# Second attention layer: QKV groups of the first chunk by half-step 5, transpositions of the second chunk in even half-steps

## The chip, the cores and the metric

The kernel runs on one core of a Trainium2 chip. The metric is device microseconds of one execution; "before" and "after" are medians of several runs on one chip. All times in this text are microseconds (us) unless another unit stands beside them.

Engine names are those of the profile: PE (matrix multiplication), DVE (vector), ACT (scalar), POOL (GpSimd), SP (the queue that issues most DMAs).

## The reference

Four layers in a row, each with a residual, on x of 2048 positions by 640 features:

```python
x = x + A(layernorm(x), wqkv, wo)      # attention
x = x + B(layernorm(x), dft matrices)  # Fourier mixing
x = x + A(layernorm(x), wqkv, wo)
x = x + B(layernorm(x), dft matrices)

def A(x, wqkv, wo):                    # 32 heads of 20 features
    q, k, v = split(x @ wqkv)
    # position s sees s, s-2, ..., s-14 (8 positions, dilation 2)
    logits = einsum("bhsd,bhswd->bhsw", q, k[idx]) * scale   # masked where idx < 0
    o = einsum("bhsw,bhswd->bhsd", softmax(logits), v[idx])
    return o @ wo

def B(x, ...):                         # real part of a DFT over features and positions
    a = x @ hid_re.T;  b = x @ hid_im.T
    return seq_re @ a - seq_im @ b
```

The weights are the same in both attention layers.

## The kernel before

Positions are split into four chunks `c` of four tiles `j` of 128 rows. The two attention layers are made by one function, `layer_a`; `first` is true in the first of them. Matrix products are made in three passes of split operands (a high part and a remainder), so each normalized tile has a high and a low half.

An attention layer is a plan of **half-steps**, from -7 to 66. One half-step computes one half (two position tiles, `jp`) of one attention unit `u`. A unit is one chunk and four heads (in the last chunk the two halves of a unit are two such sets of heads for the same two tiles): 32 units, 64 half-steps, half-step s = 2u + jp. For each, DVE multiplies Q by the eight shifted K rows (`qk_mul`, L431), POOL adds halves (L433), DVE reduces (L439) and makes the softmax with ACT's exponential (L447); three half-steps later DVE multiplies by V (`av_mul`, L469) and POOL adds the products up (L484 to L486).

PE meanwhile makes Q, K and V for later units. The work is cut in 64 **QKV groups** `g`, each of them 15 matmuls for one chunk, one quarter `q` of the heads and one tile `j` (`qkv_mm`, L362). ACT evacuates each (`qkv_evac`, L369) from one of two PSUM banks into a staging tile, of which there are two for pairs of groups; SP stores pairs to DRAM (`qkv_store`, L378 and L379), from where `w_load` (L417) and `q_load` (L401) fetch K and V windows and Q for the attention units. ACT copies Q to PSUM in each odd half-step (`q_copy`, L404).

Before a chunk's groups can run, its tiles of x are loaded (`x_load`, L195), in the first layer also reduced to mean and variance on ACT (`x_stats`, L151, L153, L170) with a power on POOL (`x_fin`, L174); then ACT normalizes (`x_norm`, L182 and L191) and PE transposes (`tp`: transposition L327, ACT's copy of the high half L331, PE's subtraction L335, ACT's copy of the low half L350). A tile of chunk c reuses the buffer of the same tile of chunk c-1, so it waits for the last group of that tile.

The order is written out by hand: `at(step, phase, fn, ...)` puts each operation into a half-step and one of some thirty phases, and the plan is issued half-step by half-step, phase by phase. Each engine, SP's queue too, works through its instructions in that order. Of the phases these matter here, in order: `peT0` (transpositions), `dma` (Q loads, x loads), `evac`, `hi`, `pe` (a group), `peL` (subtractions), `pe2` (a second group), `fin`, `red0`, `qk`, softmax phases, `exp`, `evacA`, `actL` (low halves), `evacO`, `actl` (normalizations), `av1`, `qc` (the Q copy), `actz`, `dmaw` (window loads), `dmas`, `misc`.

The half-steps of groups and transpositions come from a planner: the first 16 groups (chunk 0) from a list by hand, `LEAD0` for the first layer and `LEAD2` for the second; the others, and the half-steps `tx` of the transpositions, by a loop over half-steps with a cap on groups in each.

Between the attention layers lie the two Fourier layers, and the second attention layer begins while the first Fourier layer ends: that layer's last products (`ymm`, L1028) stand in half-steps -3 and -2.

Of the kernel before, what the change touches and what calls it, by code (L numbers as in the profile page):

```python
# [27 lines left out]
NC = 4  # L28
NJ = 4
# [13 lines left out]
LNS = ((40, 52), (40, 52))  # L43


LEAD2 = (-7, -6, -5, -4, -2, -1, 0, 0, 1, 2, 3, 4, 4, 5, 6, 7)
ZTHIRDS = (
    {49: 3, 50: 3, 51: 2, 53: 3, 54: 1, 56: 3, 57: 6, 58: 3, 59: 4, 60: 2, 61: 1, 62: 3, 63: 4, 64: 1, 55: 0, 52: 0},
    {49: 3, 50: 3, 51: 3, 52: 1, 53: 1, 54: 1, 55: 1, 56: 4, 57: 4, 58: 3, 59: 3, 60: 1, 61: 1, 62: 4, 63: 2, 64: 4},
# [25 lines left out]
def tile_layers(ctx: ExitStack, tc: tile.TileContext, x, wqkv, wo, cs, wre, wim, out):  # L75
# [166 lines left out]
    def layer_a(li, stats, handoff, prev):  # L242
        xin, xout = xs[li], xs[li + 1]
        first = li == 0
# [19 lines left out]
        def at(step, phase, fn, *args):  # L264
            plan.setdefault((step, phase), []).append((fn, args))
# [32 lines left out]
        def tp(step, kind, c, j, k0, k1, bank, col=0, tag=None):  # L298
            if step not in pieces:
                pieces[step] = []  # L300
                at(step, "peT0", pc_pe, step)
                at(step, "hi", pc_hi, step)
                at(step, "peL", pc_sub, step)
                at(step, "actL", pc_lo, step)
            pieces[step].append((kind, c, j, k0, k1, bank, col, tag))
# [387 lines left out]
        ]  # L693
        gs = list(LEAD0 if first else LEAD2)
        tx = {(0, j): -8 for j in range(NJ)}
        st = 4
        while len(gs) < NGRP:
            if (st % 2 == 0 if first or st > 10 else st > 4 and st != 6) and len(tx) < NC * NJ:
                c, j = divmod(len(tx), NJ)
                used = [i for i, x in enumerate(order) if x[0] == c - 1 and x[2] == j]  # L700
                if used[-1] < len(gs) and gs[used[-1]] < st:
                    tx[(c, j)] = st
            cap = 0 if st < 6 else 2 if st % 2 == 0 and st not in THIN[ly] else 1
            for _ in range(max(0, cap - gs[:16].count(st))):
                if len(gs) < NGRP and len(gs) <= 16 + st and tx.get(order[len(gs)][::2], st) < st:
                    gs.append(st)
            st += 1
        for g, cqj in enumerate(order):
            st = gs[g]
# [26 lines left out]
        for c in range(1, NC):  # L736
            for j in range(NJ):
                b = tx[(c, j)]
                if first or c > 1:
                    at(max(b - 4, tx.get((c, j - 2), 0)), "dma", x_load, c, j)  # L740
                else:
                    at((0, 1, 2, 3)[j], "dmas", x_load, c, j, ("xa", "xa", "xr", "ot")[j])
                if first:
                    at(b - 3, "actz", x_stats, c, j)
                    at(b - 2, "misc", x_fin, c, j)
                at(b - 1, "actl", x_norm, c, j)
                tp(b, "x", c, j, 0, 4, "xt", 0, f"s{j}")
                tp(b, "x", c, j, 4, 5, "t1", 256)
# [538 lines left out]
    st0 = [None] * NC  # L1287
    b1, b2 = LayerB(1), LayerB(3)
    layer_a(0, st0, b1, None)
    st2 = [None] * NC  # L1290
    b1.run(st2)
    layer_a(2, st2, b2, b1)
    b2.run(None)
    b2.ytile(NT - 1, 0, None)
# [56 lines left out]
```

## Time and profile before

| | |
|---|---|
| median of 3 runs | 1807.35 us (1806.6 to 1809.34) |
| the profiled execution | 1809.7 us, span of the trace 1807.9 us |
| busy: PE, DVE, ACT, POOL | 1750.4, 1387.8, 813.1, 633.4 us |
| share of the span | 97%, 77%, 45%, 35% |
| granted clock of TensorE, mean | 0.991 |
| QKV groups, both layers (L362) | 1920 matmuls, 441.3 us |
| Q copies of ACT (L404) | 64, median 431 ns |

The page's busy times are of one profiled execution. A group of instructions stands with its line, its engine, output and input tiles, and a count; in timelines the first number is the start in us from the start of the span, the second the duration, and a bracket at the end gives the idle time of the engine ahead of the instruction and what ended it. A wait for several things is put down to the last of them.

### The profile page before, as it was taken

What the parts mean: (1) busy time and instruction counts of PE and PEld (TensorE: products, weight loads), DVE (VectorE), ACT (ScalarE), POOL (GpSimd) and SP (SyncE); (2) the same over time, 40 slices, a digit from 0 to 9 for tenths busy, and PEclk for the clock granted to TensorE, in tenths of its full rate; (3) what the DMA queues carried; (4) which work ended last, traced back from release to release, by engine and by line L of the source; (5) the groups of instructions that cost most, each with busy time, mean ns of one, the idle gap of its engine ahead of it and who ended that gap; (6) DMA issues with size and microseconds to landing.
All of it is one profiled execution on the core that took longest, in us unless ns stands there. A gap on an engine that the chain in (4) does not pass through costs nothing.

```text
span 1807.9 us, 26461 instructions
## 1 busy us (share of the span) xinstructions
PE 1750.4 (97%) x8798; PEld 1508.4 (83%) x8798; DVE 1387.8 (77%) x2141; ACT 813.1 (45%) x1690; POOL 633.4 (35%) x591
## 2 busy tenths in 40 slices
PE   9999998989999999999998999999999999999999
PEld 7889887878888888888897888877787888888888
DVE  6999999787767767767736998999777676677673
ACT  4664544454445444445623334444534443443441
POOL 4889998940000000000016987999300000000000
PEclk9999998999999999999999999999999999999999
DMA  7996678758778788778645966697687776876761
GB/s 245 289 300 213 199 208 261 263 174 293 260 259 272 241 261 261 243 255 257 197 137 157 281 191 216 194 315 260 208 298 252 255 234 215 267 232 226 257 209 52
DMA packets 271849, 425.15 MB, mean 235 GB/s; under 512 B 22592, under 2 KB 150592, under 8 KB 271456
## 3 DMA queue, kind: packets, MB, share of 16 engines
q1 hardware_dynamic: 268512, 421.49, 71.8%
q10 hardware_dynamic: 3200, 1.97, 0.3%
q8 instruction: 70, 1.15, 0.3%
q14 instruction: 67, 0.55, 0.1%
HBM read 338.23 MB, written 85.14 MB: 234 GB/s over the span
## 4 chain that ended last, share of the span: by engine, by line
PE 42%; DVE 7%; DMA 5%; POOL 3%; ACT 1%; issue 1%; SPq 0%; DVEq 0%; ACTq 0%; POOLq 0%
PE aux L1028 10%; PE m L362 8%; PE t L1117 7%; PE m L1117 7%; PE pq L1117 4%; PE xt L1117 4%; DMA xc<-stg 2%; DVE pr L431 1%; DVE pr L469 1%; PE aux L509 1%; DMA win<-cs_in 1%; POOL pr L484 1%; POOL pr L433 1%; DVE lg L439 1%; POOL pr L485 0%
## 5 line engine op out<-in xcount | busy, mean ns | idle before, releaser
L362 PE MATMUL m<-r,s 128*128 128x480 f32 x1920 | 441.3, 385 | 6.9 <-ACT stg L369 4.0
L362 PEld LDWEIGHTS m<-r,s 128*128 128x128 f32 x1920 | 358.0, 190 | 63.3 <-ACT stg L369 6.0
L1110 ACT CAST r<-win 128x512 fp32r<-128x512 f32 x248 | 151.1, 619 | 172.9 <-DVE win L1146 83.6
L174 POOL TENSOR_TENSOR stats<-stats,mhalf 128x1 f32<-128x1 f32 (+1 forms) x40 | 29.8, 744 | 561.5 <-ACT stats L170 552.3
L1028 PE MATMUL aux<-r2a,zo 128*128 128x320 f32 x768 | 226.4, 310 | 0.0
L484 POOL TENSOR_TENSOR pr<-pr 128x640 f32<-128x640 f32 x126 | 204.5, 1623 | 34.9 <-DVE pr L469 34.1
L431 DVE TENSOR_TENSOR pr<-pq,win 128x1280 f32<-128x1280 f32 x128 | 189.7, 1483 | 26.6 <-ACT pq L404 26.0
L1028 PE MATMUL aux<-pr,zo 128*128 128x320 f32 x704 | 208.2, 308 | 0.0
L1111 DVE TENSOR_TENSOR r<-win,r 128x512 fp32r<-128x512 f32 x248 | 167.3, 687 | 45.6 <-ACT r L1110 44.4
L469 DVE TENSOR_TENSOR pr<-pq,win 128x1280 f32<-128x1280 f32 x128 | 190.9, 1491 | 4.3
L433 POOL TENSOR_TENSOR pr<-pr 128x640 f32<-128x640 f32 x128 | 183.2, 1431 | 29.6 <-DVE pr L431 29.3
L1117 PE MATMUL m<-r,r 128*128 128x512 f32 x606 | 157.2, 394 | 0.5 <-DVE r L1111 0.5
L1028 PEld LDWEIGHTS aux<-r2a,zo 128*128 128x128 f32 x768 | 144.2, 188 | 2.0
L1117 PEld LDWEIGHTS m<-r,r 128*128 128x128 f32 x606 | 114.0, 189 | 26.8 <-DVE r L1111 1.5
L1028 PEld LDWEIGHTS aux<-pr,zo 128*128 128x128 f32 x704 | 132.2, 188 | 2.1
L950 PE MATMUL m<-s,r 128*128 128x512 f32 x384 | 120.1, 400 | 14.1 <-DMA s<-c0b 5.5
L1117 PE MATMUL t<-r,r 128*128 128x512 f32 x483 | 131.0, 394 | 2.2 <-issue 2.2
L950 PE MATMUL t<-s,r 128*128 128x512 f32 x384 | 119.5, 399 | 2.3 <-DVE ot L1010 1.5
L485 POOL TENSOR_TENSOR pr<-pr 128x320 f32<-128x320 f32 x126 | 114.3, 907 | 9.9
L439 DVE TENSOR_REDUCE lg<-pr 128x64 f32<-128x640 f32 x128 | 103.9, 812 | 16.4 <-POOL pr L433 16.1
L1117 PEld LDWEIGHTS t<-r,r 128*128 128x128 f32 x483 | 90.6, 188 | 23.7 <-issue 3.0
L1146 DVE TENSOR_TENSOR win<-win,win 128x512 f32<-128x512 f32 x110 | 75.7, 690 | 43.9 <-DMA win<-cs_in 41.5
(284 smaller groups left out, 3228.6 us busy)
## 6 DMA issues: line engine op xcount, KB each, us to landing
win<-cs_in SPq DMA_DIRECT2D x354, 256.0 KB, 4.3
r<-xc SPq DMA_DIRECT2D x240, 256.0 KB, 4.4
win<-kvb SPq DMA_DIRECT2D x96, 440.0 KB, 4.3
xa<-cs_in SPq DMA_DIRECT2D x122, 256.0 KB, 4.1
win<-kvb SPq DMA_DIRECT2D x64, 360.0 KB, 5.3
xc<-stg SPq DMA_DIRECT2D x40, 512.0 KB, 3.6
kvb<-stg SPq DMA_DIRECT2D x60, 320.0 KB, 5.2
xr<-xs SPq DMA_DIRECT2D x41, 320.0 KB, 3.7
```

What stands on the lines that cost most here:

```text
L362: nc.tensor.matmul(mt[g][:, : 3 * F], st[:, a, k], wq[q][:, b, k], start=n == 0, stop=n == 14)
L431: nc.vector.tensor_tensor(pr, q, wview(u, jp, 0, [[1, FE]]), op=ALU.mult)
L433: nc.gpsimd.tensor_tensor(pv[:, :, 0:10], pv[:, :, 0:10], pv[:, :, 10:20], op=ALU.add)
L439: nc.vector.tensor_reduce(lgs[u][:, 2 * jp : 2 * jp + 2].rearrange("p j w h -> p (j w h)"), prq.pop((u, jp))[:, :, 0:10], axis=AX.X, op=AL ...
L469: nc.vector.tensor_tensor(pr.rearrange("p j w (h d) -> p j w h d", d=DH), lgs[u][:, 2 * jp : 2 * jp + 2].unsqueeze(4).to_broadcast([P, 2, ...
L484: g.tensor_tensor(pr[:, :, 0:4], pr[:, :, 0:4], pr[:, :, 4:8], op=ALU.add)
L485: g.tensor_tensor(pr[:, :, 0:2], pr[:, :, 0:2], pr[:, :, 2:4], op=ALU.add)
L950: self.last = nc.tensor.matmul(self.z[t][k], self.xn[c][:, a, j, k * P : (k + 1) * P], self.ct[s][:, b], start=s == 0 and i == 0, stop=s = ...
L1028: self.last = nc.tensor.matmul(self.ym[e][:, :320], zt[(k, a, ri)][:, j2 * P : (j2 + 1) * P], w[:, e * 320 : (e + 1) * 320], start=(k, a, ...
L1110: nc.scalar.copy(hi, raw)
L1111: nc.vector.tensor_tensor(lo, raw, hi.bitcast(F32), op=ALU.subtract)
L1117: nc.tensor.matmul(bank, w(a, kb), hl[b], start=start and (a, b) == (0, 0), stop=stop and (a, b) == (1, 0),)
```

## The change

```diff
-LEAD2 = (-7, -6, -5, -4, -2, -1, 0, 0, 1, 2, 3, 4, 4, 5, 6, 7)
+LEAD2 = (-7, -6, -5, -4, -2, -1, 0, 0, 1, 1, 2, 3, 3, 4, 5, 5)
...
         while len(gs) < NGRP:
-            if (st % 2 == 0 if first or st > 10 else st > 4 and st != 6) and len(tx) < NC * NJ:
+            if st % 2 == 0 and len(tx) < NC * NJ:
                 c, j = divmod(len(tx), NJ)
...
                 if first:
-                    at(b - 3, "actz", x_stats, c, j)
-                    at(b - 2, "misc", x_fin, c, j)
+                    at(b - 3, "actl", x_stats, c, j)
+                    at(b - 2, "fin", x_fin, c, j)
                 at(b - 1, "actl", x_norm, c, j)
```

In the second attention layer the planner's result becomes:

| | before | after |
|---|---|---|
| groups 8 to 15 in half-steps | 1, 2, 3, 4, 4, 5, 6, 7 | 1, 1, 2, 3, 3, 4, 5, 5 |
| transpositions of chunk 1 in | 5, 7, 8, 9 | 4, 6, 8, 10 |
| groups 16 to 25 in | 6, 8, 8, 9, 10, 10, 11, 12, 13, 14 | 6, 7, 8, 8, 9, 10, 10, 11, 12, 13 |
| groups 26 to 35 in | 14, 15, 16, 17, 18, 18, 19, 20, 21, 22 | 14, 14, 15, 16, 17, 18, 18, 19, 20, 21 |
| groups 36 to 63, other transpositions | | unchanged |

Normalizations lie one half-step ahead of a transposition and move with it; the x loads of chunk 1 stay in half-steps 0 to 3. The evacuation and the store of a group follow its half-step.

In the first attention layer groups and transpositions stay where they are. There the statistics of a tile (`x_stats`) move within their half-step from behind the Q copy to ahead of it, and the power on POOL (`x_fin`) from the end of its half-step, behind the additions, to ahead of them. This concerns the twelve tiles of chunks 1 to 3. No instruction is added or removed in either layer.

## The prediction

> **What bounds the kernel now.** I read the page first, then the chain of waits, then engine time by windows of 45 us, then the timelines of PE, DVE, ACT and the DMA queue around the edit. The edit lives in the two attention layers; the second runs from about 890 to 1290 us, and the window view shows what each engine does there against the first layer's 45 to 90 us.
>
> ```profile
> 45.00:90.00 45.00, 45.00 (x220) 38.75 (x219) 43.52 (x56) 27.86 (x67) 38.44 (x36) 1.00 0.91 288
> 950.00:995.00 45.00, 38.10 (x176) 31.76 (x176) 28.45 (x39) 15.90 (x36) 28.50 (x28) 0.96 0.51 156
> 995.00:1040.00 45.00, 44.78 (x217) 38.34 (x216) 43.64 (x58) 16.16 (x38) 42.09 (x39) 1.00 0.90 279
> 1085.00:1130.00 45.00, 45.00 (x244) 40.50 (x243) 38.14 (x58) 20.11 (x53) 35.27 (x33) 1.00 0.69 216
> ```
>
> The columns are busy us of PE, weight loads, DVE, ACT and POOL, then granted clock, DMA share and GB/s. The same work fills DVE with 43.52 of 45 us in the first layer's opening and only 28.45 of 45 in the second's (950 to 995); PE too drops there, to 38.10. After 995 DVE is full (43.64); by 1085 PE is full (45.00) and DVE sinks to 38.14. The chain of waits says who sets the end:
>
> ```profile
> 930.94 26.00 PE m L362 x120
> ...
> 1113.28 1.49 DVE pr L431
> ```
>
> From 931 on it runs over PE, mostly QKV groups (L362); at 1113 it changes to the DVE/POOL chain of the attention half-steps. So what counts for the edit is time in which PE stands still before 1113. PE's own timeline, with idle time and its releaser in brackets:
>
> ```profile
> 930.78 26.16 PE L362 MATMUL m<-r,s 128*128 128x480 f32 x120
> 957.24 3.50 PE L362 MATMUL m<-r,s 128*128 128x480 f32 x15
> 966.80 5.08 PE L362 MATMUL m<-r,s 128*128 128x480 f32 x15 [2.49 <-ACT stg L369]
> 973.40 0.66 PE L327 MATMUL xt<-ident,xa 128*128 128x128 f32 x4 [1.51 <-ACT xa L191]
> 979.34 0.66 PE L327 MATMUL xt<-ident,xr 128*128 128x128 f32 x4 [1.60 <-ACT xr L191]
> 992.62 7.64 PE L362 MATMUL m<-r,s 128*128 128x480 f32 x34 [1.25 <-ACT stg L369]
> 966.00:972.00 6.00, 5.08 (x15) 3.93 (x15) 5.15 (x7) 0.78 (x3) 5.49 (x5) 0.72 0.34 122
> ```
>
> Eight groups stream in 26.16 us (3.27 each), then PE waits 2.49, 1.51, 1.60 and 1.25 us, always for ACT (an evacuation L369, or a normalization L191 ahead of a transposition). Group 16 after the first wait takes 5.08 us, the one at 957.24 took 3.50, with the granted clock at 0.72. DVE has it worse; L431 is the QK product that opens each half-step:
>
> ```profile
> 949.46 1.49 DVE L431 TENSOR_TENSOR pr<-pq,win 128x1280 f32<-128x1280 f32 x1
> 962.13 1.49 DVE L431 TENSOR_TENSOR pr<-pq,win 128x1280 f32<-128x1280 f32 x1 [3.39 <-ACT pq L404]
> 979.64 1.49 DVE L431 TENSOR_TENSOR pr<-pq,win 128x1280 f32<-128x1280 f32 x1 [8.32 <-ACT pq L404]
> 992.94 1.49 DVE L431 TENSOR_TENSOR pr<-pq,win 128x1280 f32<-128x1280 f32 x1 [4.09 <-ACT pq L404]
> 1002.05 1.48 DVE L431 TENSOR_TENSOR pr<-pq,win 128x1280 f32<-128x1280 f32 x1
> ...
> 1077.09 0.49 DVE L159 SCALAR_TENSOR_TENSOR xr<-aux,xr 128x320 f32<-128x320 f32 x1 [1.98 <-PE aux L509]
> 1113.28 1.49 DVE L431 TENSOR_TENSOR pr<-pq,win 128x1280 f32<-128x1280 f32 x1 [1.50 <-ACT pq L404]
> ```
>
> These are half-steps 4, 6, 8, 10, 12, then two later rows. DVE stands 3.39 + 8.32 + 4.09 = 15.8 us, each time for L404, ACT's copy of Q. The reason stands on ACT, which works in order:
>
> ```profile
> 961.00 0.59 ACT L350 CAST s<-xt 128x512 fp32r<-128x512 f32 x1 [2.77 <-PE xt L335]
> 961.64 0.45 ACT L404 COPY pq<-qs 128x320 f32<-128x320 f32 x1
> ```
>
> L350 is the second evacuation of a transposition; it waits 2.77 us for PE's subtraction (L335), which stands behind a whole QKV group. The Q copy is issued in odd half-steps, and before the change the transpositions of chunk 1 sit in 5, 7, 9 (and 8): the copy queues behind L350, and DVE behind the copy.
>
> **The change, second layer.** I worked out the planner's list by hand from its code. After it, groups 9 to 15 lie one half-step earlier (15 two), transpositions of chunk 1 in 4, 6, 8, 10, and groups 17, 19, 20, 22 to 25 and most up to 35 one half-step earlier; from half-step 22 on the list is the old one. No instruction is added or removed; PE has the same work, in another order.
>
> What is removed: with the transpositions in even half-steps, L350's wait falls into a half-step without a Q copy, and group 15 no longer stands behind the transposition of (1,1). I walked PE and ACT through the new list with the durations above. PE enters at group 6 at 934.05 (930.78 + 3.27) and every bank it needs is evacuated, and every tile normalized, before PE arrives, with 0.5 us or more to spare, up to the transposition of half-step 20. So the four waits go: 2.49 + 1.51 + 1.60 + 1.25 = 6.85 us. The slow group goes too: 5.08 - 3.50 = 1.58. Together **8.4 us off PE's stretch**.
>
> The clock term is where a rule is weighed. The row: 2.49 us of waiting were followed by a group at granted clock 0.72. By the Trainium skill (TensorE: Matmul & The Clock Gate, "HAM oscillation") PE drops to the slow clock only after gaps above some 3.4 us, and by that rule the 1.58 us were not this gap's and would stay, the saving then being 6.85 us. The trace disagrees, so the sum keeps the term.
>
> What is late next. DVE's 15.8 us do not all come off: in my walk half-step 12 starts at 994.2 instead of 1002.05 (7.9 us earlier), since PE is the bound from half-step 1 on. From 1002 to 1060 DVE goes at its own pace and only then falls behind PE (waits such as 1.98 us for PE at 1077.09, 1.50 for ACT at 1113.28), so PE's 8.4 and DVE's 7.9 arrive at half-step 34 nearly together; I take 8.4, PE being what ended last there. Behind 1113 the list is unchanged and the shift passes to the end.
>
> What is added: in half-steps 1 and 3 two groups stand where one stood. Their evacuations come ahead of the exponential on ACT, and the store of group 9 comes ahead of the load of the next K window on the DMA queue, which is in order as well:
>
> ```profile
> 944.88 0.43 SPq L417 DMA_DIRECT2D win<-kvb  x1
> 947.78 0.37 SPq L378 DMA_DIRECT2D kvb<-stg  x1
> 46.23 0.64 SPq L417 DMA_DIRECT2D win<-kvb  x1
> 52.11 1.49 DVE L431 TENSOR_TENSOR pr<-pq,win 128x1280 f32<-128x1280 f32 x1 [0.21 <-DMA win<-kvb]
> ```
>
> The second-layer window load issued at 944.88, ahead of group 9's store at 947.78; with the new list it comes behind it, as in the first layer, where the load issued at 46.23 and the product waited for it until 52.11. I expect half-step 4 at about 954 instead of 949.46, 4.5 us late. I cost this at nothing, because in that stretch PE has queued groups to work on (it does not wait for half-step 4 before group 13's bank, evacuated by then) and DVE regains it in half-steps 6 to 10 where 15.8 us of waits lay. If that cover is gone, it costs up to 4.5. Store and evacuation of the staged pairs keep their two buffers: each is reused two pairs later, 6.5 us (2 x 3.27) on at the least.
>
> **The change, first layer.** The planner gives the same list there. What moves are the statistics of x: two ACT passes from behind the Q copy to ahead of it, and the POOL power (L174) from the end of the half-step to its start. Twelve tiles each.
>
> ```profile
> 51.21 0.43 ACT L404 COPY pq<-qs 128x320 f32<-128x320 f32 x1 [1.09 <-DVE pr L469]
> 51.57 0.73 ACT L151 ACTIVATE junk<-xa 128x640 bf16<-128x640 f32 x1
> 53.39 0.20 ACT L170 ACTIVATE stats<-stats 128x1 f32<-128x1 f32 x1
> 71.23 0.30 ACT L182 ACTIVATE stats<-stats 128x1 f32<-128x1 f32 x1 [0.39 <-POOL stats L174]
> 72.39 0.42 ACT L404 COPY pq<-qs 128x320 f32<-128x320 f32 x1
> 73.80 1.47 DVE L431 TENSOR_TENSOR pr<-pq,win 128x1280 f32<-128x1280 f32 x1
> 173.88 0.30 ACT L182 ACTIVATE stats<-stats 128x1 f32<-128x1 f32 x1 [3.22 <-POOL stats L174]
> 176.02 1.48 DVE L431 TENSOR_TENSOR pr<-pq,win 128x1280 f32<-128x1280 f32 x1
> 170.13 0.38 SPq L195 DMA_DIRECT2D xa<-x_in  x1
> DMA to landing us min/median/max: 2.8/3.7/6.3
> ACT stats L182 <- POOL stats L174: 9.9, 7, 3.2
> ACT pq L404 <- DVE pr L469: 6.0, 3, 2.9
> PE xt L335 <- ACT s L331: 2.4, 3, 0.8
> ```
>
> One tile's statistics take ACT from 51.57 to 53.59, 2.02 us. DVE is the full engine here, so whatever delays L404 past its cover delays the kernel. Half-step 3: ACT idles 1.09 us ahead of the copy, so the copy comes 0.93 later; it ended at 51.64 and the next product started at 52.11, cover 0.47, cost 0.46. Half-step 7: no idle but 0.39 us of waiting for POOL's power, which now comes earlier and no longer holds ACT; copy 1.63 later, cover 73.80 - 72.81 = 0.99, cost 0.64, of which the 0.46 already lost is not paid again: 0.2. Half-step 27: POOL held ACT for 3.22 us, which covers the statistics, but x is issued only at 170.13 and lands 3.7 later at the median, 173.8; statistics until 175.9, copy until 176.3, and the product that started at 176.02 about 0.5 late with the hand-over. At the other nine places idle time ahead of the copy (6.0 us in 90 to 200 us) and POOL waits that go (9.9) leave nothing above 0.15. Sum: **+1.2 us**. Bounds: if the loads land at 6.3 instead of 3.7, half-step 27 costs 2.6 more, and half-step 7 its full 0.64: about +3.7; on the other side PE's waits of 2.4 us for the transposition copies, which stand behind the statistics today, go: -2.4 if PE counted there, but DVE has no wait for PE in that stretch, so I take the value near the DVE rows. POOL has the same work; its power comes ahead of one addition (L433) instead of ahead of the next.
>
> **Sum.** The profiled execution took 1809.7 us (span 1807.9): 1809.7 - 8.4 + 1.2 = 1802.5. The median of the runs shown is 2.35 us below that execution, so in medians 1807.35 - 7.2 = **1800.2 us**.
>
> **Rivals.** (a) DVE is the true pace of 950 to 1113, and PE only looks full. Then all 15.8 us come off: 1807.35 - 15.8 + 1.2 = 1792.8. For it: 43.64 of 45 us of DVE in 995 to 1040. Against it: DVE's waits for PE after 1060. The Trainium skill (Perfetto Trace Analysis, "Identifying the Most-Contended Engine") judges PE by weight-load time instead of matmul time; by that rule PE had room (38.34 and 40.50 of 45), which would speak for this rival; the 0.22 us per matmul in the stream show no such room. Chance 0.08.
> (b) The early lateness is not regained: half-step 4's 4.5 us stay, because ACT's copies, now behind two evacuations, keep DVE that far behind PE until PE's banks run out. 1807.35 - 8.4 + 4.5 + 1.2 = 1804.7, within 0.2% of before (3.6 us, about what a measurement here can tell). Chance 0.13.
> (c) Slower: in the first layer the statistics ahead of the copy find no cover at all, because each x lands as late as the slowest row. Place: ACT, odd half-steps 1 to 31; price: 12 x 2.02 = 24.2 less the covers behind the copy, 0.47 to 0.99, some 0.7 x 12 = 8.4, that is 15.8: 1807.35 - 8.4 + 15.8 = 1814.8. It decides from about 1.0 us per tile ((8.4 + 3.6) / 12). Against it: of the places I could follow, only one waits for its load. Chance 0.09.
> That the change does not do what it says I exclude: the two planner lists differ as described.
>
> **How the numbers follow.** Forecast 0.70, rivals 0.08, 0.13, 0.09. The range leaves out (c) and the far half of (a): low 1796.0, about midway between the forecast without first-layer loss (1799.0) and (a); high 1806.0, (b) with 1.3 more of the first layer's bounds. Faster by over 0.2%: 0.70 + 0.08, less 0.03 for the edge of the forecast: 0.75; within 0.2%: 0.13 + 0.03 = 0.16; slower 0.09.
>
> **What would show it.** Right: between 934 and 1000 PE has no idle rows and no granted clock below 1; the L404 waits at half-steps 6 and 8 are gone, and half-step 12 starts some 8 us earlier against the layer's first product; half-step 4 starts later than before; the first layer's products from half-step 28 on are 0.5 to 2 us later, and L182 no longer waits for POOL. Wrong: PE waits for ACT in half-steps 1 to 10; or the products at half-step 34 gain much less than those at 12 (the gain was DVE's only); or DVE waits for L404 in the first layer at more than three places.

## The result, and the profile after

| | before | after |
|---|---|---|
| median (4 runs each, same chip) | 1807.38 us (1806.6 to 1809.34) | 1794.91 us (1792.42 to 1796.94) |
| ratio | | 0.9929, 95% interval 0.9911 to 0.9947 |
| the profiled execution, its span | 1809.7 us, 1807.9 us | 1796.79 us, 1795.0 us |
| busy: PE, DVE, ACT, POOL | 1750.4, 1387.8, 813.1, 633.4 us | 1745.0, 1384.8, 813.7, 632.9 us |

Faster by 12.5 us; 1800.2 was forecast with a range from 1796.0. The sign was right, the size was not, and the time lies 1.1 us outside the range. The windows that answer to those of before follow. Half-step 4 of the second layer comes at nearly the same time (950.38 us, 949.46 before), so its window stays 950 to 995. The two behind it are shifted by 12.3 us, since half-step 12 comes 10.3 us earlier and half-step 34 12.6:

```profile
45.00:90.00 45.00, 45.00 (x221) 39.04 (x220) 42.11 (x56) 27.45 (x66) 37.81 (x34) 1.00 0.88 284
950.00:995.00 45.00, 45.00 (x221) 39.07 (x220) 39.04 (x52) 17.35 (x40) 38.51 (x36) 1.00 0.72 226
982.70:1027.70 45.00, 45.00 (x217) 38.97 (x217) 42.86 (x59) 16.57 (x38) 41.27 (x39) 1.00 0.86 276
1072.40:1117.40 45.00, 45.00 (x244) 40.46 (x243) 38.11 (x57) 20.15 (x53) 35.29 (x33) 1.00 0.67 216
```

From 950 to 995 PE is full where it had 38.10 of 45, the granted clock is 1.00 where it was 0.96, and DVE does 39.04 us of work instead of 28.45. PE's timeline of the second layer's opening, with the first idle time that it shows behind 928.48:

```profile
928.48 26.14 PE L362 MATMUL m<-r,s 128*128 128x480 f32 x120
954.93 3.50 PE L362 MATMUL m<-r,s 128*128 128x480 f32 x15
965.57 3.54 PE L362 MATMUL m<-r,s 128*128 128x480 f32 x15
972.54 0.60 PE L327 MATMUL xt<-ident,xr 128*128 128x128 f32 x4
1161.82 0.82 PE L335 MATMUL t<-s,nident 128*128 128x256 f32 x2 [0.92 <-ACT s L331]
```

From 928.48 on no PE row has a bracket until 1161.82; the four waits for ACT are gone, and so is the group of 5.08 us. DVE's timeline, a step of the softmax (L460) ahead of half-step 4 and the products (L431) of half-steps 4, 6, 8, 10, 12 and 34:

```profile
945.73 0.38 DVE L460 TENSOR_REDUCE pq<-lg 128x16 f32<-128x128 f32 x1 [2.53 <-ACT lg L447]
950.38 1.49 DVE L431 TENSOR_TENSOR pr<-pq,win 128x1280 f32<-128x1280 f32 x1 [0.79 <-DMA win<-kvb]
961.09 1.49 DVE L431 TENSOR_TENSOR pr<-pq,win 128x1280 f32<-128x1280 f32 x1 [1.07 <-ACT pq L404]
971.59 1.49 DVE L431 TENSOR_TENSOR pr<-pq,win 128x1280 f32<-128x1280 f32 x1 [0.96 <-ACT pq L404]
981.85 1.49 DVE L431 TENSOR_TENSOR pr<-pq,win 128x1280 f32<-128x1280 f32 x1 [1.06 <-ACT pq L404]
991.74 1.49 DVE L431 TENSOR_TENSOR pr<-pq,win 128x1280 f32<-128x1280 f32 x1 [0.67 <-ACT pq L404]
1100.65 1.49 DVE L431 TENSOR_TENSOR pr<-pq,win 128x1280 f32<-128x1280 f32 x1 [1.50 <-ACT pq L404]
```

The waits of 3.39, 8.32 and 4.09 us at half-steps 6, 8 and 10 are now 1.07, 0.96 and 1.06. Ahead of half-step 4 DVE now waits 2.53 us for ACT's exponential (L447), which stands behind the evacuation of a second group, and 0.79 us for its K window, which on the SP queue stands behind the store of group 9:

```profile
945.51 0.37 SPq L378 DMA_DIRECT2D kvb<-stg  x1
946.54 0.57 SPq L417 DMA_DIRECT2D win<-kvb  x1
```

To see where the 12.9 us of the two spans went I use the starts of L431, the first product of each half-step, in the two traces. Half-step 63 of the first attention layer starts at 368.09 before and 365.01 after: 3.1 us gained there. Half-step 0 of the second starts at 933.88 and 931.59, so the Fourier layer between gave back 0.8. From there to half-step 63 the second layer takes 332.72 (933.88 to 1266.60) and 322.28 us (931.59 to 1253.87): 10.4 us gained. The rest, to the end of the span, takes 541.3 and 541.1 us. So 3.1 - 0.8 + 10.4 + 0.2 = 12.9.

In the first layer the grouped rows of DVE from 40 to 210 us, of before and then of after, show what changed; the columns are busy us, mean ns of one, and idle time ahead with its releasers:

```profile
L431 DVE TENSOR_TENSOR pr<-pq,win 128x1280 f32<-128x1280 f32 x34 | 50.4, 1483 | 1.1 <-ACT pq L404 0.6 <-DMA win<-kvb 0.6
L563 DVE TENSOR_TENSOR r2a<-zo,r2a 128x640 fp32r<-128x640 f32 x4 | 6.6, 1638 | 0.0
L919 DVE TENSOR_TENSOR zo<-zo 128x512 fp32r<-128x512 f32 x4 | 5.4, 1354 | 0.0
```

```profile
L431 DVE TENSOR_TENSOR pr<-pq,win 128x1280 f32<-128x1280 f32 x34 | 50.4, 1483 | 1.8 <-ACT pq L404 1.8
L563 DVE TENSOR_TENSOR r2a<-zo,r2a 128x640 fp32r<-128x640 f32 x4 | 4.5, 1133 | 0.0
L919 DVE TENSOR_TENSOR zo<-zo 128x512 fp32r<-128x512 f32 x4 | 3.8, 955 | 0.0
```

The waits ahead of L431 grew by 0.7 us, which is the loss that was forecast (1.2). But eight subtractions that the diff does not touch (L563 splits a weight, L919 a Fourier matrix, into high part and remainder) became 2.0 + 1.6 = 3.6 us shorter. Together that is -2.9 of the 3.1.

### The profile page after: what moved, and what is told of

Its sections match the earlier page's. It is cut to its first block, busy times and chain, and to the rows that moved or that the text cites. A ratio compares the mean times of both kernels' runs of the same rounds, so it can differ in the third digit from the quotient of the medians.

```text
span 1795.0 us, 26464 instructions
## 1 busy us (share of the span) xinstructions
PE 1745.0 (97%) x8798; PEld 1508.6 (84%) x8798; DVE 1384.8 (77%) x2141; ACT 813.7 (45%) x1690; POOL 632.9 (35%) x591
## 4 chain that ended last, share of the span: by engine, by line
PE 60%; DVE 14%; POOL 11%; DMA 8%; issue 3%; ACT 2%; SPq 0%; DVEq 0%; ACTq 0%; POOLq 0%
PE aux L1028 13%; PE m L362 11%; PE m L1117 10%; PE t L1117 10%; PE pq L1117 5%; PE xt L1117 5%; POOL pr L484 3%; DVE pr L431 3%; POOL pr L433 3%; DVE pr L469 3%; DMA win<-cs_in 2%; PE aux L509 2%; POOL pr L485 2%; DMA xc<-stg 2%; PE m L950 1%
## 5 line engine op out<-in xcount | busy, mean ns | idle before, releaser
L484 POOL TENSOR_TENSOR pr<-pr 128x640 f32<-128x640 f32 x126 | 206.2, 1636 | 35.2 <-DVE pr L469 34.8
L431 DVE TENSOR_TENSOR pr<-pq,win 128x1280 f32<-128x1280 f32 x128 | 189.8, 1483 | 16.5 <-ACT pq L404 15.2
L433 POOL TENSOR_TENSOR pr<-pr 128x640 f32<-128x640 f32 x128 | 183.3, 1432 | 16.1 <-DVE pr L431 15.6
L369 ACT COPY stg<-m 128x480 f32<-128x480 f32 x128 | 71.0, 555 | 94.6 <-PE m L362 73.4
```

Of the source, the lines that this page charges most:

```text
L431: nc.vector.tensor_tensor(pr, q, wview(u, jp, 0, [[1, FE]]), op=ALU.mult)
L433: nc.gpsimd.tensor_tensor(pv[:, :, 0:10], pv[:, :, 0:10], pv[:, :, 10:20], op=ALU.add)
L484: g.tensor_tensor(pr[:, :, 0:4], pr[:, :, 0:4], pr[:, :, 4:8], op=ALU.add)
```

## The experiments

The time of the second layer is compared as the distance from its half-step 0 to its half-steps 12, 34 and 63, since its start moves by several us from trace to trace with the Fourier layer ahead of it:

| kernel | median us (runs) | ratio to before, 95% interval | first layer: half-step 63 at | second layer: 0 to 12 | 0 to 34 | 0 to 63 |
|---|---|---|---|---|---|---|
| before | | | 368.09 | 68.17 | 179.40 | 332.72 |
| after | 1794.91 (4) | 0.9929 (0.9911 to 0.9947) | 365.01 | 60.15 | 169.06 | 322.28 |
| e1_second_only | 1796.96 (5) | 0.994 (0.9927 to 0.9952) | 368.12 | 60.15 | 169.07 | 322.46 |
| e2_first_only | 1804.24 (8) | 0.9981 (0.9969 to 0.9992) | 365.63 | 69.73 | 181.01 | 334.21 |
| e3_power_only | 1806.9 (10) | 0.999 (0.9979 to 1.0) | 367.01 | 66.56 | 177.81 | 331.02 |
| e4_stats_only | 1812.22 (10) | 1.0027 (1.0018 to 1.0037) | 373.13 | 69.67 | 180.94 | 334.24 |
| e5_groups_only | 1804.72 (10) | 0.9963 (0.9947 to 0.9979) | 365.24 | 66.61 | 177.70 | 331.04 |
| e6_transp_only | 1799.9 (4) | 0.9925 (0.9901 to 0.9948) | 366.24 | 52.34 | 163.48 | 324.08 |
| e7_pool_shift | 1815.46 (1) | one run | 369.16 | 68.14 | 179.32 | 332.72 |
| e9_thin_26_30 | 1796.81 (6) | 0.9904 (0.9883 to 0.9924) | 366.50 | 60.14 | 161.82 | 321.62 |

The kernel before took 1808.23 us on the chip of e1 to e4 and 1812.09 on that of e5 to e9, so ratios are to be compared, not times. The last four columns are read from one trace of each kernel.

The second layer is the same, instruction for instruction, in before, e2, e3, e4 and e7, and yet it takes 331.02 to 334.24 us. PE has the same four waits in all five (2.45 to 2.49, 1.51, 1.60 and 1.25 us); what differs is how often the granted clock is low behind them. In e3 it is 1.00 all the way from 934 to 1010, and the group behind the longest wait takes 3.51 us. In e2 two groups are slow. PE's rows of e3, then of e2:

```profile
966.93 3.51 PE L362 MATMUL m<-r,s 128*128 128x480 f32 x15 [2.45 <-ACT stg L369]
```

```profile
962.94 5.10 PE L362 MATMUL m<-r,s 128*128 128x480 f32 x15 [2.49 <-ACT stg L369]
976.30 5.09 PE L362 MATMUL m<-r,s 128*128 128x480 f32 x15
```

Before and e7 have one such group, e4 two. The layer takes 331.02 us with none, 332.72 with one, 334.2 with two: some 1.6 us each. So a gain in the second layer is to be held against 331.0 to 334.2 us, and what is left of it without the clock against e3.

**The two layers apart.** e1 takes only the second layer's lines of the diff, e2 only the first layer's.

> The planner's two edits alone (second layer); the first layer's statistics stay where they were. Theory A, PE's stretch alone pays: the whole gain of 12.5 us is the second layer's and what follows; about 1795 us. Theory B, the first layer's 3.1 us reach the end: about 1798 us, and the first layer's last product starts at 368.1 as before. The sum of the prediction without its first-layer loss: 1799. In every theory half-step 12 of the second layer lies about 8 us and half-step 34 about 10 us nearer to that layer's first product.

> The first layer's edits alone: statistics ahead of the Q copy, power ahead of the addition. Theory A: no gain at the end, 1807 us within 1. Theory B: 1804.3 us. The prediction's term: 1808.6. In the trace the first layer's last product should start near 365.0 instead of 368.1; what counts is how much of this is left at the first residual addition of the Fourier layer, 427.5 before and 428.2 after the change.

e1 is 11.3 us below before, e2 4.0 us. The second layer of e1 takes 322.46 us like that of after, and its first layer is that of before (368.12); e2 has the shorter first layer. The time of e1 alone does not decide between the two theories; e2's does, since its interval leaves out 1: the first layer's gain reaches the end, and the theory that it is swallowed by PE behind falls. At half-step 34 of the first layer the eight traces with its whole edit lie between 202.4 and 203.1 us, before and e1 at 205.5.

**The first layer's two moves apart.**

```diff
# e3: at(b - 2, "fin", x_fin, c, j)      and x_stats left in "actz"
# e4: at(b - 3, "actl", x_stats, c, j)   and x_fin left in "misc"
```

> Only the power on POOL moves. Port theory: DVE's subtractions between two buffers of the on-chip memory (L919, L563) wait for a POOL instruction under way; the power moved ahead of the addition shifts POOL by 0.55 us and DVE hits a shorter wait. Then this kernel has nearly the whole first-layer gain: half-step 34 near 202 instead of 205.5, the two L563 of 2.2 us fall to about 1.2. Rival, ACT theory: the gain is from normalizations no longer waiting for POOL; then too the gain is here, but L563 stays at 2.2 and the waits for L404 shrink instead.

> Only the statistics on ACT move. The prediction's reasoning: DVE waits for the Q copy at half-steps 4, 6, 8 and 28, 0.5 to 0.7 us each, half-step 34 at 206 to 207 instead of 205.5, time within 1.5 us of before. Rival: ACT's earlier evacuations pay and half-step 34 comes at 203 or earlier.

Half-step 63 comes 1.1 us earlier with the power alone, 5.0 later with the statistics alone, and 3.1 earlier with both (2.5 in e2). The two do not add up, and both expectations missed the size: half-step 34 came at 204.40 in e3 (near 202 was expected) and at 210.49 in e4 (206 to 207). The grouped DVE row of e4 shows why the statistics alone lose:

```profile
L431 DVE TENSOR_TENSOR pr<-pq,win 128x1280 f32<-128x1280 f32 x32 | 47.5, 1484 | 6.4 <-ACT pq L404 5.6 <-DMA win<-kvb 0.8
```

DVE waits 5.6 us for the Q copy instead of 0.6. ACT's grouped rows of L182, the first step of the normalization, from 40 to 210 us, of before, of e4 and of after, tell what holds the copy:

```profile
L182 ACT ACTIVATE stats<-stats 128x1 f32<-128x1 f32 x12 | 3.6, 301 | 10.8 <-POOL stats L174 10.8
```

```profile
L182 ACT ACTIVATE stats<-stats 128x1 f32<-128x1 f32 x12 | 3.5, 295 | 15.1 <-POOL stats L174 15.1
```

```profile
L182 ACT ACTIVATE stats<-stats 128x1 f32<-128x1 f32 x12 | 3.7, 311 | 0.0
```

In e4 the statistics stand ahead of the copy, and the normalization ahead of both waits 15.1 us for a power that POOL makes at the end of the half-step. With the power early, that wait is gone, ACT is free sooner, and the statistics fit. The subtractions L563 fell in e3 and after (4.5 us for the four) and not in e4 (6.5): they follow the power's place on POOL, not the statistics.

**Why an untouched subtraction gets shorter.** Theory P: a DVE subtraction with both inputs in SBUF and a POOL instruction hold each other up, and the power ahead of the additions only shifted POOL's additions against DVE. e7 is the kernel before with a power on a scratch tile at that place, and the true one left at its old place:

```diff
+        def pool_shift():
+            nc.gpsimd.tensor_tensor(shiftt, shiftt, mhalf[:, :1], op=ALU.pow)
...
                     at(b - 2, "misc", x_fin, c, j)
+                    at(b - 2, "fin", pool_shift)
```

> The kernel before, with one more POOL instruction: at the place where the edit puts the power (ahead of the addition L433, in the half-steps of the first layer's statistics), a power on a 128x1 scratch tile whose result nobody reads; the true power stays at the end of the half-step. Theory P (a DVE subtraction with both inputs in SBUF and a POOL instruction hold each other up, and the edit only shifted POOL's additions against DVE): the subtractions L563 of half-steps 14 and 16 fall from 2.2 us to about 1.2, and L563's median from 1.75 to about 1.2, with the true power and the statistics left where they were. Rival (they became shorter since the power itself left the end of the half-step): L563 stays at 2.2 us there and its median at 1.7 or more.

The median of the four L563 fell from 1750 to 1220 ns, and at half-steps 14 and 16 to 1.22 us each, with the statistics and the power where they were before. Theory P stands. The grouped rows of e7 (L926 there is L919, seven lines further down):

```profile
L563 DVE TENSOR_TENSOR r2a<-zo,r2a 128x640 fp32r<-128x640 f32 x4 | 5.3, 1314 | 0.0
L926 DVE TENSOR_TENSOR zo<-zo 128x512 fp32r<-128x512 f32 x4 | 4.2, 1038 | 0.0
```

They save 1.3 + 1.2 us, but the shift does not save time by itself: POOL has twelve instructions of 0.55 us more, DVE's waits for POOL's L433 grow from 12.1 to 14.5 us in the layer, and half-step 63 comes 1.1 us later than before. So e7 shows what shortens the subtractions; that the shorter subtractions are the layer's gain rests on the rows of before and after.

**The second layer's two lines apart.** Both have the first layer's edit in full. e5 takes the new list of the first 16 groups with the old rule (transpositions of chunk 1 in 5, 7, 8, 9), e6 the new rule with the old list (transpositions in 6, 8, 10, 12, groups 16 to 47 up to two half-steps later).

> The first layer's edit in full, and of the second layer's edit only the list of the first 16 groups; the old rule puts the transpositions of chunk 1 into half-steps 5, 7, 8, 9. Theory G (the gain comes from the groups standing earlier, PE being the pace): the gain nearly stays, some 1796 to 1798 us, PE without idle rows between 934 and 1000. Theory T (what pays is that the second evacuation of a transposition, L350, no longer stands ahead of a Q copy in an odd half-step): DVE still waits 3 us or more for L404 at half-steps 6 and 8, half-step 12 comes less than 4 us earlier against half-step 0, and the run takes 1800 us or more.

> The first layer's edit in full, and of the second layer's edit only the transpositions' half-steps; with the old list of 16 groups the planner puts the transpositions of chunk 1 into 6, 8, 10 and 12. Theory T: DVE's waits for L404 at half-steps 6 to 10 fall under 2 us each and most of the gain is here, some 1797 us. Theory G: group 15 still stands in half-step 7 and chunk 1's groups come later, so PE waits for its transpositions; half-step 12 gains little or nothing, 1802 us or more. With both parts needed, each alone gives under half of the 10 us of the second layer.

e5 gains 1.7 us in the layer against before and nothing against e3 (331.04 and 331.02 us): the groups alone bring little, and DVE still waits 3.31, 1.94 and 5.71 us for the Q copy at half-steps 6, 8 and 10. PE's timeline of e5 shows three waits close together, and the windows show the clock, which is low already behind the first of them (1.51 us) and stays low in the group behind the last:

```profile
969.48 0.66 PE L327 MATMUL xt<-ident,xa 128*128 128x128 f32 x4 [1.51 <-ACT xa L191]
970.80 0.80 PE L335 MATMUL xt<-s,nident 128*128 128x512 f32 x1 [0.56 <-ACT s L331]
973.26 1.11 PE L327 MATMUL xt<-ident,xr 128*128 128x128 f32 x4 [1.55 <-ACT xr L191]
974.24 4.97 PE L362 MATMUL m<-r,s 128*128 128x480 f32 x15
```

```profile
970.00:972.00 2.00, 1.14 (x5) 0.50 (x2) 1.63 (x2) 1.11 (x3) 1.66 (x2) 0.64 0.26 102
974.00:976.00 2.00, 2.00 (x8) 1.72 (x7) 1.93 (x4) 0.76 (x2) 0.94 (x2) 0.50 0.71 210
```

e6 is the telling one. By half-step 12 it is 15.8 us ahead of before (52.34 against 68.17): DVE's waits for the Q copy at half-steps 6, 8 and 10 are gone. At half-step 34 it is still 15.9 ahead, at half-step 46 only 9.2 and at 63 8.6 (324.08 against 332.72). PE has no idle time from 1035 to 1160, and DVE gives its lead back to PE:

```profile
1035.00:1160.00 125.00, 125.00 (x670) 112.71 (x669) 106.03 (x157) 53.12 (x133) 101.47 (x93) 1.00 0.63 197
```

```profile
1107.46 0.49 DVE L159 SCALAR_TENSOR_TENSOR xr<-aux,xr 128x320 f32<-128x320 f32 x1 [1.96 <-PE aux L509]
1129.89 0.49 DVE L159 SCALAR_TENSOR_TENSOR xr<-aux,xr 128x320 f32<-128x320 f32 x1 [1.93 <-PE aux L509]
```

Part of that lead was PE's work put off: the planner of e6 has two groups fewer ahead of half-step 34 and second groups in 34 and 38 instead, and two groups in a stream take 6.7 us (97.3 us for 29, below). So theory T is right that the transpositions' half-steps carry most of the gain (8.6 of 10.4 against before, 6.9 of 8.7 against e3, which like e6 has no slow group; the ratio to before cannot be told from that of the kernel after), and yet DVE's lead is not what arrives at the end.

**A better list?** e9 takes the kernel after and lets only one group into half-steps 26 and 30, where DVE waits for PE; the second groups move to 34 and 38.

```diff
-THIN = (..., (12, 16, 20, 24, 28, 32, 36, 44, 48))
+THIN = (..., (12, 16, 20, 24, 26, 28, 30, 32, 36, 44, 48))
```

> The kernel after, with half-steps 26 and 30 of the second layer capped at one group: the groups of 26 to 37 come one half-step later (one or two from 30), doubles stand in 34 and 38, chunk 3's transpositions in 30, 32, 34, 36 instead of 28 to 34; the last group stays in 47. Theory PE (in half-steps 26 to 34 PE paces DVE, which waits some 7 us there in the profile after, and from 34 on DVE and POOL are the pace): up to 7 us of these waits go, less what returns at 34 to 38; 1789 to 1793 us. Rival (the groups are only put off, and PE becomes the pace at 34 to 38): same time as after, 1794 to 1796, with waits of DVE for L404 or for PE moved to half-steps 34 to 40.

Its DVE is at half-step 34 another 7.2 us earlier than after's (161.82 against 169.06), and at 63 only 0.7 (321.62 against 322.28). The ratio, 0.9904, looked better than after's, so the two ran once more on one chip, with a third that thins half-step 26 only.

> The kernel after, unchanged, beside the two thinned lists on the same chip. By the earlier runs: 12 to 13 us below the kernel before; within the second layer (half-step 0 to half-step 63) 10.4 us below it.

> The kernel after with half-steps 26 and 30 of the second layer capped at one group, again. Theory PE total (PE has no idle time from 930 us to its last group in both kernels, so an earlier DVE at half-step 34 is given back by 46): 0 to 1 us below the kernel after, not to be told from it, half-step 34 some 7 us earlier within the layer, half-step 63 at most 1 earlier. Rival (the lead at half-step 34 is worth something at the end): 3 us or more below the kernel after.

> The kernel after with only half-step 26 of the second layer capped at one group (its second group moves to half-step 34, chunk 3's transpositions to 30, 32, 34, 36). Theory PE total: within 1 us of the kernel after at half-step 63, with a lead of 2 to 5 us at half-step 34 that is given back by 46. Rival: half of the second kernel's gain, 1.5 us or more below the kernel after.

| on one chip, before 1811.07 us | median us (6 runs) | ratio, 95% interval | second layer 0 to 34 | 0 to 63 |
|---|---|---|---|---|
| r1_after_again | 1797.04 | 0.9924 (0.9909 to 0.9938) | 169.07 | 322.26 |
| r2_thin_again | 1794.56 | 0.9907 (0.9892 to 0.9923) | 162.36 | 321.56 |
| r3_thin_26 | 1796.01 | 0.9918 (0.9904 to 0.9932) | 164.88 | 322.61 |

Within the layer the thinned lists differ from after by -0.7 and +0.35 us at half-step 63 although they lead by 6.7 and 4.2 at half-step 34, where they have put off two groups and one. What sets the end is when PE is through with its groups. PE's last group of before, then of after:

```profile
1177.30 3.44 PE L362 MATMUL m<-r,s 128*128 128x480 f32 x15
```

```profile
1164.68 3.44 PE L362 MATMUL m<-r,s 128*128 128x480 f32 x15
```

Half-step 63 starts at 1266.60 and 1253.87, 85.9 and 85.8 us behind the end of that group. It is 85.7 to 85.9 in all the kernels here but e6 (86.5), whatever lead DVE had at half-step 34.

The intervals of the three overlap, so there is no shown winner over the kernel after. But r2's median lies 2.5 us below r1's, between what the two theories expected, and e9's ratio too is the lower one; the layer's traces show 0.7 us of it. A gain of some 2 us is neither shown nor excluded.

## Why the prediction was right and wrong

**Right: the bound and the mechanism of the second layer.** PE's stand-still set the gain; its waits for ACT, the slow group and DVE's waits for L404 went as described. Half-step 12 was forecast 7.9 us earlier; it came 68.17 - 60.15 = 8.0 earlier. That close a match is partly luck, since the old list alone puts half-step 12 between 66.56 and 69.73 us. Half-step 4 was forecast 4.5 us late and is 3.2 late against the layer's start (18.79 against 15.58 us); only 0.79 us of that is the wait for the window behind the store, on which the forecast put its weight, and 2.53 us the wait for the exponential, whose place behind the second evacuation it named without a price. By half-step 8 it is regained (40.00 against 45.76), so rival (b) fell.

**Wrong in size: "8.4 us off PE's stretch".** It measured 10.4 (10.3 in e1). The sum took the idle rows and one slow group. PE's grouped row for the groups from its first group to the transposition of half-step 20, before (930.78 to 1037.48) and after (928.48 to 1028.20, one group more):

```profile
L362 PE MATMUL m<-r,s 128*128 128x480 f32 x420 | 96.2, 386 | 4.0 <-ACT stg L369 4.0
```

```profile
L362 PE MATMUL m<-r,s 128*128 128x480 f32 x435 | 97.3, 381 | 0.0
```

Before, 28 groups at after's price would take 97.3 x 28/29 = 93.9 us, not 96.2: slower groups cost 2.3 us, not 1.58. In e3, with the same waits and no low clock, they take 94.6 us, so 0.7 of the 2.3 is not the clock's, and which step of PE makes it no trace here shows. PE's idle rows there make 4.0 + 1.5 + 1.6 = 7.1, not 6.85 (a wait of 0.22 at 1015.96 was left out). That explains 9.4 of the 10.4; the remaining 1.0 lies in the short pieces around the stops and stays open. Held against e3 the gain of the layer is 331.02 - 322.28 = 8.7 us, where the sum without its clock term had 6.85.

**Right in the trace of before, but not certain: the clock term.** With the waits gone the granted clock is 1.00 in all four windows, and e5 shows a low clock without a long wait: it is down behind a gap of 1.51 us, and behind gaps of 0.56 and 1.55 us more a group takes 4.97 us at 0.50. But the same four waits cost the term twice in e2 and e4, once in before and e7 and not at all in e3, so the forecast took from one trace, as sure, what comes in some executions and not in others. The rule of some 3.4 us in the Trainium skill (TensorE: Matmul & The Clock Gate, "HAM oscillation") differs from the traces with a low clock, whose longest gap is 2.49 us, and the traces decide here.

**Wrong in sign: "+1.2 us" for the first layer.** It measured -3.1. Half of the step held: the waits ahead of L431 grew by 0.7, with waits for L404 of 0.49, 0.68 and 0.64 us at half-steps 4, 6 and 8. But its half-step 27 term (+0.5, with a bound of +2.6) did not appear: DVE has no wait for L404 after half-step 8. There the load was issued at 166.00 instead of 170.13, and though the statistics began 5.4 us behind it (3.7 was taken), the copy ended just as the product started at 173.82. L182, which had waited for POOL, no longer does, as said. What the step lacked is the 3.6 us of shorter subtractions, and so the products from half-step 28 on are not 0.5 to 2 us later, as forecast, but 2.2 us earlier. It said of POOL only that it "has the same work; its power comes ahead of one addition": true, and the shift was put at nothing, though L563's 816 to 2235 ns for one shape stood in the trace of before. The lower bound, -2.4, was set by PE's waits and for another reason.

**Rival (a)** gave 1792.8, nearer to 1794.91 than my forecast, and it is still the wrong mechanism: in e6 DVE is 15.8 us ahead at half-step 12 and keeps 8.6. **Rival (c)**, slower since the statistics find no cover, did not come. e4 comes nearest to it, at 5.0 us instead of 15.8, and for another reason: there the copy is held by L182's wait for the late power, not by loads that land late.

**The sum, repaired:** 1809.7 - 10.4 - 3.1 + 0.8 - 0.2 = 1796.8, the profiled execution. Of the miss, 4.3 us are the first layer's sign and 2.0 the second layer's size; the Fourier layer's 0.8 and the tail's 0.2 are within what runs differ by. Part of the second layer's 2.0 is so too, since the old list alone spreads over 3.2 us; the first layer's sign is not.

## What to carry to other kernels

Add up the bound engine's stand-still with the slow restart behind each stop, not the idle rows alone; and before you count a lead of another engine as gain, look whether the bound engine has idle time left to give, for here 15.8 us of DVE's lead ended as 8.6. Do not price a slow restart from one trace alone: here the same code showed it not at all, once or twice. Where one instruction shape shows a spread of durations, ask what ran beside its long ones: an edit that only shifts another engine by half a microsecond can move that price. Two moves of one edit may be worth -1.1 and +5.0 alone and -3.1 together, so cost them together where one hides the wait of the other.

## What the hardware showed that I had not expected

A DVE subtraction with two SBUF inputs and a POOL addition exclude each other, and the one that starts first wins. Before, POOL's L484 starts 0.03 us ahead of DVE's L919:

```profile
55.86 2.09 DVE L919 TENSOR_TENSOR zo<-zo 128x512 fp32r<-128x512 f32 x1
55.83 1.57 POOL L484 TENSOR_TENSOR pr<-pr 128x640 f32<-128x640 f32 x1
```

After, the power has delayed POOL, and DVE is first:

```profile
55.93 0.78 DVE L919 TENSOR_TENSOR zo<-zo 128x512 fp32r<-128x512 f32 x1
56.11 2.04 POOL L484 TENSOR_TENSOR pr<-pr 128x640 f32<-128x640 f32 x1
```

DVE's instruction takes 0.78 instead of 2.09 us, and now POOL's takes 2.04 instead of 1.57. In e3 POOL is 0.03 us ahead once more, and the long form is back although the power is early there too:

```profile
56.40 2.08 DVE L919 TENSOR_TENSOR zo<-zo 128x512 fp32r<-128x512 f32 x1
56.37 1.57 POOL L484 TENSOR_TENSOR pr<-pr 128x640 f32<-128x640 f32 x1
```

The weight's subtraction at half-step 14 shows the amount. Before, it starts 0.02 us behind L484 and takes 2.23:

```profile
108.92 2.23 DVE L563 TENSOR_TENSOR r2a<-zo,r2a 128x640 fp32r<-128x640 f32 x1
108.90 1.57 POOL L484 TENSOR_TENSOR pr<-pr 128x640 f32<-128x640 f32 x1
```

After, it meets only the end of POOL's L433, and L484 comes behind it:

```profile
108.71 1.22 DVE L563 TENSOR_TENSOR r2a<-zo,r2a 128x640 fp32r<-128x640 f32 x1
107.82 1.42 POOL L433 TENSOR_TENSOR pr<-pr 128x640 f32<-128x640 f32 x1
109.20 2.16 POOL L484 TENSOR_TENSOR pr<-pr 128x640 f32<-128x640 f32 x1
```

L563's shortest row takes 0.82 us. After, POOL's L433 ends at 109.24 and the subtraction at 109.93; before, L484 ends at 110.47 and the subtraction at 111.15. Both times the subtraction ends 0.68 to 0.69 us behind POOL's instruction, whenever it started: it does nearly all of its work behind it. So it is in before, after, e3, e4 and e7 with every L563 and L919 that starts while POOL's L433 or L484 is under way: L563 ends 0.68 to 0.69 us behind the last POOL addition that started ahead of it, L919 0.55 to 0.61. The Trainium skill (SBUF — State Buffer, "Who interferes with whom") states that a DVE instruction with two SBUF inputs contends with a GpSimd instruction that reads SBUF, by way of a read interface that the two share, and that the order of issue decides which of them blocks. These rows agree with that order; that it is the interface and nothing else, no run here shows.

Open is how e3's 1.1 us come about in detail: its subtractions L563 are 2.0 us shorter and its L919 0.8, but its first product starts 0.4 us later, and from 40 to 210 us DVE waits 0.7 us more for ACT's L126 (1.1 against 0.4) and 0.5 more for the window load (1.1 against 0.6). And the Fourier layer between the two attention layers differs by some 3 us between kernels that are equal there. The clock is not the cause: e2 and e6 have a granted clock of 1.00 in it and take 564.4 and 567.3 us from half-step 63 to half-step 0. What is stays open.
